# GeGLU down products of both sequence halves in the second pass, with the first half's hidden tiles stored in HBM

## The chip, the cores and the metric

The kernel runs on one core of one Trainium2 chip. The metric is the device time of one launch in microseconds (us). The kernel before takes 787.78 us, the median of 3 runs (787.53 to 787.96). The profile is of one further execution.

## The reference

The input x has 2048 rows of 512 numbers. It is normalized row by row, and two branches are added to it: a Fourier mixing written as products with DFT matrices, and a gated feed-forward layer (GeGLU) with 1792 hidden columns.

```python
    a = jnp.einsum("bsd,ed->bse", x, dft_hid_re)
    b = jnp.einsum("bsd,ed->bse", x, dft_hid_im)
    y = jnp.einsum("ts,bse->bte", dft_seq_re, a) - jnp.einsum("ts,bse->bte", dft_seq_im, b)
    ...
    g = jnp.einsum("bsd,df->bsf", x, w_gate)
    u = jnp.einsum("bsd,df->bsf", x, w_up)
    h = _gelu(g) * u
    return jnp.einsum("bsf,fd->bsd", h, w_down)
    ...
    return x + _A_ref(xn, ...) + _B_ref(xn, ...)
```

Everything is fp32.

## The kernel before

Each fp32 operand is split into two parts in a reduced fp32 format, a high part (a copy on ScalarE, line 295, tile names ending in h) and a low part (a subtraction on VectorE, line 300, names ending in l). A product is then three matmuls (`mm3`, line 311): high by high and the two mixed ones. Block products are done by a scheme with seven products in place of eight (numbered 0, 1, 4, 5, 6, 2, 3), whose results pass through PSUM banks in a chain: products accumulate in a bank, the bank's running sum is copied out by ScalarE (`copy`, line 1620), and a later product goes on accumulating in the same bank. A full matmul is 128 by 128 by 512, and a `W` of the code, one product of a unit, is six of them.

The first half of the program makes the Fourier branch (tiles named z, m, y). The second half, `units`, makes the feed-forward layer in 28 units. Unit n makes gate columns (n even) or up columns (n odd) of pair q = n // 2, 256 hidden columns for one half of the sequence: units 0 to 13 are the first pass (rows 0 to 1023), units 14 to 27 the second pass (rows 1024 to 2047). A unit has banks a, b and c. Product 5 accumulates in b, ScalarE copies b to a side tile q6, product 6 accumulates in b, ScalarE copies b to a side tile w, and product 3 closes b. In the first pass an even unit also makes inner products, `X` (three matmuls each, banks b2 and c2), which both passes share; they are written to HBM (`m_park`) and start the second pass's banks from there.

When a pair's gate and up blocks are there, ScalarE applies the gelu (`gate`, line 747) and VectorE multiplies (`up_1`, line 752): four hidden tiles s per pair. From these, VectorE and ScalarE form the seven operands of the down product (`hl`, names hh, hl, hth, htl). The down weights of pair q (`wd`, loaded at line 677) are summed (`weight_sums`, line 642) and split in the same way, for each q of 0 to 13, though q and q + 7 use the same weights.

Down products (`down_op`, tiles dn) are small PE jobs of three matmuls for each pair q in them. `TURNS` says which pairs are multiplied together in one bank: `[[0], [1, 2], [3, 4], [5, 6], [7, 8, 9], [10, 11], [12, 13]]`. When a turn's last pair is ready, its 14 jobs go to a list `todo`, and `fill` places them between the products of the units that follow, at the places that `order(n)` marks with d0 to d3. A finished dn bank is copied by ScalarE to a tile `part` (line 1704) and added to an HBM tensor `partial` by a DMA on GpSimd's queue (line 1707). The last turn (`last_down`) starts its banks from `partial` and stores the output.

The order of the PE's instructions is the order in which `add` is called with engine "p". A planner in the kernel (class `Plan`) places the other engines' operations around it, by assumed costs and by the room in a pool of 109 tiles of 128 by 512 fp32 in SBUF (`SLOTS`) and 8 PSUM banks.

```python
            if lead(n - 1, 4):
                return "5 Y43 1 d1 Y42 d2 6 d0 3 d3 2"
            if fetched(n, 4):
                return "5 1 d2 6 d0 3 d1 2 d3"
```

These strings give the order in a unit: digits are products, X and Y inner products (Y42 and Y43 are the last two of the unit ahead), d a place for down jobs. The first is that of an odd unit of the first pass, the second that of a unit of the second pass.

Of the kernel before, what the change touches and what calls it, by code (L numbers as in the profile page):

```python
# [261 lines left out]
def fnet_geglu_kernel(ctx: ExitStack, tc: tile.TileContext, x, xt, cs, dh, wgu, wd, out):  # L262
# [81 lines left out]
    m_park = dram.tile([2, NP, 2, P, CH], F32, name="m_park")  # L344
    x_park = dram.tile([2, 2, P, CH], F32, name="x_park")
# [976 lines left out]
    TURNS = [[0], [1, 2], [3, 4], [5, 6], [7, 8, 9], [10, 11], [12, 13]]  # L1322
    INNER_AHEAD = 2
    INTO_ACC = (6, 3)
# [27 lines left out]
    def unit_at(n):  # L1352
        return TU + n * 14.25
# [76 lines left out]
    def units():  # L1430

        def weights(m):
            name, at = m if isinstance(m, tuple) else (0, m)
            if short(m):
                add(("lw", m), "s", .9, lambda: load_short(m), mb=MB, makes={("wx", m): 1})
            else:
                add(("lw", m), "s", .9, lambda: load_w(m) if isinstance(m, int) else load_wd(m[1]), mb=2 * MB, makes={("wx", m): 2},
                    ahead=W_AHEAD if (m if isinstance(m, int) else 2 * m[1]) < NP - 2 else None)
# [41 lines left out]
        for q in range(NP):  # L1480
            weights(("d", q))
# [200 lines left out]
        def down_op(qs, r, js):  # L1682
            sp, key = qs[0] // (NP // 2), (qs[0], r, js[0])
            tiles = {}

            def f():
                for j in js:
                    tiles[j] = ps_tile("dn")
                    down_product(qs, r, j, tiles[j])
            k = {0: 0, 1: 0, 4: 1, 5: 1, 6: 2, 2: 2, 3: 3}[r]  # L1690
            add(("dn", *key), "p", 3 * MM * len(js) * len(qs), f,
                after=[("lo", ("w", ("d", q), k)) for q in qs] + [("lo", ("h", q, r)) for q in qs],
                uses=[("wl", ("d", q), k) for q in qs] + [("hl", q, r) for q in qs], banks=[("dn", qs[0], r, j) for j in js],
                holds=[("dn", qs[0], r, j) for j in js])
            for j in js:
                if qs == TURNS[-2] and r in INTO_ACC:
                    add(("dc", qs[0], r, j), "v", V5, lambda j=j: nc.vector.tensor_add(acc[r, j], tiles[j], acc[r, j]),
                        after=[("dn", *key), ("la", 2, r, j)], uses=[("acc", 2, r, j)], holds=[("dn", qs[0], r, j)])
                    continue
                part = {}  # L1700

                def cp(j=j, part=part):
                    part[0] = slot("part")
                    nc.scalar.activation(part[0], tiles[j], AF.Copy)  # L1704
                add(("dc", qs[0], r, j), "a", A5, cp, after=[("dn", *key)], makes={("part", qs[0], r, j): 1}, holds=[("dn", qs[0], r, j)])
                sent = [("da", qs[0] - 1, r, j)] if qs[0] % (NP // 2) else [("lys", 3, j)] if sp and r == 3 else []
                add(("da", qs[-1], r, j), "g", .6, lambda j=j, part=part: nc.gpsimd.dma_start(partial[sp, r, j], part[0], accum_op=OP.add),  # L1707
                    after=[("dc", qs[0], r, j), *sent], uses=[("part", qs[0], r, j)], mb=MB, adds=True)

        def more(q):  # L1710
            for qs in TURNS[:-1]:
                if q == qs[-1]:
                    todo.extend(("d", qs, r, [j]) for r in D_ORDER for j in range(2))
                    return [2 * t[-1] + 2 for t in TURNS if t[-1] > q][0]
# [6 lines left out]
        def hidden(n, blk, ready, src, holds, uses):  # L1721
# [5 lines left out]
            add(("f", n, blk), "v", V5, lambda: up_1(n, blk, src()), after=[*ready, ("f", n - 1, blk)], holds=holds, uses=[*uses, s], soon=2 if holds else SOON)  # L1727
            if blk in H_USE:
                r = H_USE[blk]
                add(("hi", ("h", q, r)), "a", A5, lambda: up_2(n, blk), after=[("f", n, blk)], uses=[s], makes={("hl", q, r): 2})  # L1730
                add(("lo", ("h", q, r)), "v", V5, lambda: up_3(n, blk), after=[("hi", ("h", q, r))], uses=[s, ("hl", q, r)])

        def hidden_sums(q):
            s = [("s", q, blk) for blk in H_PLACE]
            n = 2 * q + 1
            f = [("f", n, blk) for blk in H_PLACE]
            for k, (after, uses) in enumerate((([f[0], f[1]], [0, 1]), ([("hs", q, 0), f[3], ("lo", ("h", q, 2))], [3, 1]),
                                               ([("hs", q, 1), ("lo", ("h", q, 0))], [3, 0]), ([("hs", q, 1), f[2], ("lo", ("h", q, 1))], [2, 3]))):
                add(("hs", q, k), "v", V5, lambda k=k: h_sum(q, k), after=after, uses=[s[u] for u in uses])
# [3 lines left out]
        for q in range(NP - 1):  # L1743
            hidden_sums(q)

        turn = 4

        def order(n):
# [14 lines left out]
        for n in range(U1):  # L1763
            if n % 2 == 0:
                turn = more(n // 2 - 1) or turn
            wanted = -(-len(todo) // (turn - n))
# [12 lines left out]
            for u in order(n).split():  # L1779
                if u[0] == "d":  # L1780
# [4 lines left out]
                else:  # L1785
                    mult(n, int(u))
# [10 lines left out]
                    elif u == "2":  # L1797
                        sums("aq", n, "q6", "c", [("p", n, 2), ("q6", n)], c)
                        hidden(n, (0, 1), [("aq", n)], lambda n=n: side[n, "q6"], [], [("q6", n)])
# [3 lines left out]
        def last_down(qs):  # L1803

            sp, tiles, p0 = NC // 2 - 1, {}, {}
            given = TURNS[-2]

            def step(r, j, *h):
                k, sl = (r, j, *h), slice(h[0] * HD, (h[0] + 1) * HD) if h else slice(CH)
                hold, a = ("dn", "z", *k), ("acc", 2, r, j)  # L1810

                def seed():
                    tiles[k] = ps_tile("dn")[:, :HD if h else CH]
                    nc.scalar.activation(tiles[k], acc[r, j][:, sl], AF.Copy)
                add(("es", *k), "a", A2 if h else A5, seed, after=[("la", 2, r, j), ("dc", given[0], r, j)], uses=[a], banks=[hold], holds=[hold])
                w = {0: 0, 1: 0, 4: 1, 5: 1, 6: 2, 2: 2, 3: 3}[r]
                add(("e", *k), "p", (1.5 if h else 3) * MM * len(qs), lambda: down_product(qs, r, j, tiles[k], True, sl),
                    after=[("es", *k)] + [("lo", ("w", ("d", q), w)) for q in qs] + [("lo", ("h", q, r)) for q in qs],
                    uses=[("wl", ("d", q), w) for q in qs] + [("hl", q, r) for q in qs], holds=[hold])
                done, u = ("zd", *k), ("p0", j)  # L1820
# [10 lines left out]
                if r == 0:  # L1831
                    def first():
                        p0[j] = slot("p0")
                        nc.scalar.activation(p0[j], tiles[k], AF.Copy)
                    drain(first, [], [], {u: 1}, "a", A5)
                elif r == 2:
                    drain(lambda: nc.scalar.activation(acc[2, j], tiles[k], AF.Copy), [], [a], (), "a", A5)
                elif r == 1:
                    drain(lambda: nc.vector.tensor_add(acc[1, j], tiles[k], p0[j]), [("zd", 0, j)], [a, u])
                    put((0, 0), lambda: acc[1, j], a, done)  # L1840
                elif r == 5:
                    drain(lambda: plus(p0[j]), [("zd", 1, j)], [u])
                    add(("z5", j), "v", V5, lambda: nc.vector.tensor_add(acc[2, j], acc[2, j], p0[j]), after=[done, ("zd", 2, j)],
                        uses=[u, ("acc", 2, 2, j)])
                elif r == 4:
                    drain(lambda: plus(acc[2, j]), [("z5", j)], [("acc", 2, 2, j)])
                    put((0, 1), lambda: acc[2, j], ("acc", 2, 2, j), done)
                elif r == 6:
                    drain(lambda: plus(p0[j]), [("z5", j)], [u])
                    add(("z6", j), "v", V5, lambda: nc.vector.tensor_add(acc[4, j], tiles[4, j], p0[j]), after=[done, ("e", 4, j)],  # L1850
                        uses=[u, ("acc", 2, 4, j)], holds=[("dn", "z", 4, j)])
                    put((1, 1), lambda: acc[4, j], ("acc", 2, 4, j), ("z6", j))
                elif not h:
                    drain(lambda: plus(p0[j]), [("z6", j)], [u])
                    put((1, 0), lambda: p0[j], u, done)
                else:
                    def end():
                        nc.vector.tensor_add(p0[j][:, sl], tiles[k], p0[j][:, sl])
                        (nc.sync if h[0] else nc.scalar).dma_start(out[2 + j, 2 * sp, :, sl], p0[j][:, sl])
                    drain(end, [("z6", j)], [u], (), "v", V2)  # L1860

            for r in D_ORDER[:-1]:
                for j in range(2):
# [77 lines left out]
```

## Time and profile before

| what | value |
|---|---|
| median of 3 runs | 787.78 us |
| the profiled execution's own time | 787.55 us |
| span from the first to the last instruction | 785.8 us |
| PE busy | 781.2 us, 99% |
| VectorE (DVE) busy | 743.7 us, 95% |
| ScalarE (ACT) busy | 555.8 us, 71% |
| matmuls | 3441 |
| HBM read, written | 127.14 MB, 74.73 MB |

Busy time of a PE is modelled, since matmuls overlap: a row gives a matmul 0.39 us, while the next one starts sooner. The start times of successive matmuls tell the pace. The profiled time is 1.75 us above its span, and 0.23 us below the median.

### The profile page before, as it was taken

Reading aid. Unit: us, or ns where it says so; the run is one execution under the profiler, and the core shown is the slowest. Engines: PE = TensorE matmul, PEld = TensorE weight load, DVE = VectorE, ACT = ScalarE, POOL = GpSimd, SP = SyncE. Lnnn points to the kernel's source line nnn. Section 1 sums busy time; section 2 is a strip of 40 time slices with the busy share of each in tenths; the row PEclk is TensorE's granted clock in tenths of the full one; section 3 lists DMA queues with packets and bytes.
Section 4 is the critical chain, followed back from the end, with each engine's and each line's share of the span. In section 5 each row is a group of like instructions: output and inputs, shape, how many; then the busy total and the mean of one; then the engine's idle time right before and its main releaser. Section 6 shows DMA issues by size and latency. Waiting matters only on the chain.

```text
span 785.8 us, 11798 instructions
## 1 busy us (share of the span) xinstructions
PE 781.2 (99%) x3441; PEld 644.3 (82%) x3441; DVE 743.7 (95%) x1415; ACT 555.8 (71%) x1057; POOL 177.5 (23%) x268
## 2 busy tenths in 40 slices
PE   9999999999999999999999999999999999999998
PEld 6888888888888888888888888888888888888886
DVE  7999999999899899999999998999999999999986
ACT  6997555666545374766777776787787898878863
POOL 0110520043221042000222431343322212222200
PEclk9999999999999999999999999999999999999999
DMA  9976997779999879982765986697799984999952
GB/s 331 388 192 171 367 352 267 248 278 273 359 371 373 315 297 375 393 315 84 197 216 137 209 187 150 121 314 153 200 255 348 290 208 81 283 324 247 247 131 108
DMA packets 103377, 199.52 MB, mean 254 GB/s; under 512 B 12272, under 2 KB 21520, under 8 KB 103120
## 3 DMA queue, kind: packets, MB, share of 16 engines
q1 hardware_dynamic: 75600, 129.81, 47.8%
q0 software_dynamic: 27424, 68.70, 35.6%
q8 instruction: 27, 0.44, 0.2%
q14 instruction: 38, 0.31, 0.1%
q10 hardware_dynamic: 288, 0.26, 0.1%
HBM read 127.14 MB, written 74.73 MB: 257 GB/s over the span
## 4 chain that ended last, share of the span: by engine, by line
PE 96%; DMA 1%; issue 1%; POOL 1%; ACT 0%; DVE 0%; POOLq 0%; ACTq 0%
PE m L311 35%; PE b L311 19%; PE dn L311 16%; PE y L311 10%; PE c L311 7%; PE a L311 5%; PE z L311 4%; DMA partial<-part 1%; DMA x<-in_x 0%; POOL partial L1707 0%; POOL xT_hl L625 0%; POOL m_park L1628 0%; ACT part L1704 0%; DVE bn L378 0%; ACT q L1620 0%
## 5 line engine op out<-in xcount | busy, mean ns | idle before, releaser
L295 ACT ACTIVATE psh<-pan 128x512 fp32r<-128x512 f32 x203 | 118.0, 625 | 73.7 <-DVE pan L587 23.2
L300 DVE TENSOR_TENSOR psl<-pan,psh 128x512 fp32r<-128x512 f32 x198 | 128.6, 681 | 0.3 <-ACT psh L295 0.2
L1707 POOL DMA_DIRECT2D partial<-part x80 | 69.5, 876 | 187.1 <-ACT part L1704 147.0
L311 PE MATMUL m<-psh,xcl 128*128 128x512 f32 x232 | 90.2, 389 | 0.0
L311 PE MATMUL m<-psh,xch 128*128 128x512 f32 x232 | 90.2, 389 | 0.0
L311 PE MATMUL m<-psl,xch 128*128 128x512 f32 x232 | 90.2, 389 | 0.0
L1704 ACT ACTIVATE part<-dn 128x512 f32<-128x512 f32 x80 | 47.3, 594 | 17.4 <-PE dn L311 16.8
L311 PEld LDWEIGHTS m<-psh,xch 128*128 128x128 f32 x232 | 43.6, 188 | 9.1
L311 PEld LDWEIGHTS m<-psh,xcl 128*128 128x128 f32 x232 | 43.5, 188 | 9.1
L311 PEld LDWEIGHTS m<-psl,xch 128*128 128x128 f32 x232 | 43.6, 188 | 8.9
L300 DVE TENSOR_TENSOR wl<-ws,wh 128x512 fp32r<-128x512 f32 (+1 forms) x70 | 46.3, 671 | 3.3 <-ACT wh L295 3.2
L295 ACT ACTIVATE wh<-ws 128x512 fp32r<-128x512 f32 (+1 forms) x70 | 42.3, 615 | 0.6 <-DVE ws L642 0.6
L552 POOL DMA_DIRECT2D partial<-part x28 | 20.7, 765 | 95.6 <-ACT part L548 81.1
L587 DVE TENSOR_TENSOR pan<-pan 128x512 f32<-128x512 f32 x58 | 38.8, 682 | 2.6 <-DMA pan<-in_cs 2.6
L311 PE MATMUL m<-psh,xa 128*128 128x512 f32 x116 | 40.4, 389 | 0.0
L300 DVE TENSOR_TENSOR htl<-s,hth 128x512 fp32r<-128x512 f32 x56 | 37.8, 685 | 2.2 <-ACT hth L295 2.2
L1620 ACT ACTIVATE w<-b 128x512 f32<-128x512 f32 x42 | 25.1, 599 | 18.8 <-PE b L311 17.8
L1058 POOL DMA_DIRECT2D t_park<-pan x29 | 16.1, 556 | 95.0 <-DVE pan L588 84.1
L765 DVE TENSOR_TENSOR s<-s 128x512 f32<-128x512 f32 x56 | 37.3, 684 | 0.1
L1620 ACT ACTIVATE q<-b 128x512 f32<-128x512 f32 x42 | 25.1, 597 | 15.7 <-PE b L311 13.9
L295 ACT ACTIVATE hth<-s 128x512 fp32r<-128x512 f32 x56 | 33.8, 627 | 1.4 <-DVE s L765 1.3
L311 PE MATMUL dn<-hth,wh 128*128 128x512 f32 x84 | 32.7, 389 | 0.0
(761 smaller groups left out, 2424.5 us busy)
## 6 DMA issues: line engine op xcount, KB each, us to landing
pan<-in_cs SPq DMA_DIRECT2D x157, 256.0 KB, 6.3
partial<-part POOLq DMA_DIRECT2D x108, 256.0 KB, 5.6
wx<-in_wgu SPq DMA_DIRECT2D x48, 256.0 KB, 5.3
t_park<-pan POOLq DMA_DIRECT2D x29, 256.0 KB, 5.9
pan<-t_park SPq DMA_DIRECT2D x29, 256.0 KB, 5.9
wd<-in_wd SPq DMA_DIRECT2D x28, 256.0 KB, 5.8
m<-m_park SPq DMA_DIRECT2D x28, 256.0 KB, 6.4
acc<-partial SPq DMA_DIRECT2D x28, 256.0 KB, 4.6
```

What stands on the lines that cost most here:

```text
L295: nc.scalar.activation(t[0], src, AF.Copy, scale=float(sign))
L300: engine.tensor_sub(t[1], src, hi)
L311: nc.tensor.matmul(ps, a[u][:, sl], b[v], start=first and r == 0, stop=last and r == 2, skip_group_check=resumed)
L552: nc.gpsimd.dma_start(partial[sp, r, j], ypart.pop((r, j)), **({} if r in (0, 5, 6) else {"accum_op": OP.add}))
L587: return [lambda: nc.vector.tensor_sub(t3, b22, b12), lambda: nc.vector.tensor_sub(t1, b12, b11), lambda: (nc.vector.tensor_sub(b22, *((t1 ...
L765: nc.vector.tensor_sub(t, u, v)
L1058: plan.add(("park", i), "g", .6, lambda: nc.gpsimd.dma_start(t2_park[c, k], pan_src[i][5]), after=[("S", i, 2)], mb=MB, uses=[("r", i, b22)])
L1620: nc.scalar.activation((bank if banks else side)[(n, to, *more)], src(), AF.Copy)
L1704: nc.scalar.activation(part[0], tiles[j], AF.Copy)
L1707: add(("da", qs[-1], r, j), "g", .6, lambda j=j, part=part: nc.gpsimd.dma_start(partial[sp, r, j], part[0], accum_op=OP.add), after=[("dc" ...
```

## The change

All down products are made in the second pass. `TURNS` now names pairs of weights, `[[0, 1], [2, 3], [4, 5, 6]]`, and a turn's jobs are made for both halves of the sequence (q = p and q = p + 7) from one prepared set of weights. The first pass writes its 28 hidden tiles s to HBM (`h_park`, GpSimd's queue) as soon as they are multiplied, and the second pass loads them again (SP's queue) and forms the operands there. Units 4 to 18 have no down jobs to place; turn 0 starts at unit 19, turn 1 at unit 23, and the last turn, 28 jobs for three pairs, follows unit 27. The strings of `order` are changed for odd units of the first pass and for the second pass (z is product 2 of the unit ahead). A planner's function for due times (`unit_at`) and the separate final sums of the first half are replaced to match.

```diff
+    h_park = dram.tile([NP // 2, 4, P, CH], F32, name="h_park")
...
-            mm3(ps, wl[("d", q), r], cols(j), [t[:, part] for t in hl[q, r]], q == qs[0] and not seeded, q == qs[-1],
+            mm3(ps, wl[("d", q % (NP // 2)), r], cols(j), [t[:, part] for t in hl[q, r]], q == qs[0] and not seeded, q == qs[-1],
...
-    TURNS = [[0], [1, 2], [3, 4], [5, 6], [7, 8, 9], [10, 11], [12, 13]]
+    TURNS = [[0, 1], [2, 3], [4, 5, 6]]
+    BEGIN = [4, 19, 23]
...
-        for q in range(NP):
+        for q in range(NP // 2):
             weights(("d", q))
...
+            if n < NP:
+                add(("hp", q, blk), "g", .6, lambda: nc.gpsimd.dma_start(h_park[q, H_PLACE.index(blk)], hs[q, blk]), after=[("f", n, blk)],
+                    uses=[s], mb=MB)
+
+                def get():
+                    hs[q, blk] = slot("s")
+                    nc.sync.dma_start(hs[q, blk], h_park[q, H_PLACE.index(blk)])
+                add(("hg", q, blk), "s", .45, get, after=[("hp", q, blk)], makes={("s2", q, blk): 1}, mb=MB)
...
             if lead(n - 1, 4):
-                return "5 Y43 1 d1 Y42 d2 6 d0 3 d3 2"
+                return "5 Y43 d1 6 1 d2 3 d0 Y42 " + "2 " * (n < NP - 1) + "d3"
...
             if fetched(n, 4):
-                return "5 1 d2 6 d0 3 d1 2 d3"
+                return "5 1 d2 6 " + "z " + "d0 3 d1 d3" + " 2" * (n == U1 - 1)
...
-            if n % 2 == 0:
-                turn = more(n // 2 - 1) or turn
-            wanted = -(-len(todo) // (turn - n))
+            if n in BEGIN[1:]:
+                t = BEGIN.index(n) - 1
+                todo.extend(("d", t, sp, r, j) for r in D_ORDER for sp in range(2) for j in range(2))
+            wanted = -(-len(todo) // (min(b for b in (*BEGIN, U1) if b > n) - n))
...
+            for r in (0, 2, 1, 5):
+                for sp in range(2):
+                    for j in range(2):
+                        step(r, sp, j)
...
+        while todo:
+            fill()
         last_down(TURNS[-1])
```

Three places show how instructions move. Buffer numbers stand behind the names.

The first is PE in unit 4, an even unit of the first pass (a, c: banks of its outer products; xT00, xT40, xT01: inputs of inner products; dn: a down job). Before:

```order
L311 MATMUL a_5221<-xT00h_3971,wh_5118 128x512
L311 MATMUL a_5221<-xT00l_3972,wh_5118 128x512
L311 MATMUL a_5221<-xT00h_3971,wl_5119 128x512
L311 MATMUL c_5227<-xT40h_4160,wh_5130 128x512
L311 MATMUL c_5227<-xT40l_4161,wh_5130 128x512
L311 MATMUL c_5227<-xT40h_4160,wl_5131 128x512
L311 MATMUL dn_5236<-hth_5110,wh_5072 128x512
L311 MATMUL dn_5236<-hth_5110,wl_5073 128x512
L311 MATMUL dn_5236<-htl_5111,wh_5072 128x512
L311 MATMUL a_5221<-xT01h_3982,wh_5118 128x512
```

And now:

```order
L311 MATMUL a_5170<-xT00h_3978,wh_5073 128x512
L311 MATMUL a_5170<-xT00l_3979,wh_5073 128x512
L311 MATMUL a_5170<-xT00h_3978,wl_5074 128x512
L311 MATMUL c_5177<-xT40h_4117,wh_5078 128x512
L311 MATMUL c_5177<-xT40l_4118,wh_5078 128x512
L311 MATMUL c_5177<-xT40h_4117,wl_5079 128x512
L311 MATMUL a_5170<-xT01h_4000,wh_5073 128x512
L311 MATMUL a_5170<-xT01l_4001,wh_5073 128x512
```

Bank a is copied by ScalarE between its third matmul and its fourth. The down job that stood there is gone: three matmuls on another bank are left between the two. It is so in units 4, 6, 8, 10 and 12.

The second is PE in unit 5, an odd unit (b: the bank of products 5, 6 and 3). Before, the rows ahead of these are the last of product 5 on b, three of b2 (inner product 3) and the first five of product 1 (on the bank b2 of its own):

```order
L311 MATMUL b2_5233<-xT11h_4112,wl_5248 128x512
L311 MATMUL dn_5465<-hth_5325,wh_5012 128x512
L311 MATMUL dn_5465<-hth_5325,wl_5013 128x512
L311 MATMUL dn_5465<-htl_5326,wh_5012 128x512
L311 MATMUL c2_5339<-xT41h_4702,wih_5267 128x512
L311 MATMUL c2_5339<-xT41l_4703,wih_5267 128x512
L311 MATMUL c2_5339<-xT41h_4702,wil_5268 128x512
L311 MATMUL dn_5482<-hth_5325,wh_5012 128x512
L311 MATMUL dn_5482<-hth_5325,wl_5013 128x512
L311 MATMUL dn_5482<-htl_5326,wh_5012 128x512
L311 MATMUL b_5387<-xT60h_4147,wh_5350 128x512
```

And now, from the last of product 5 to the first of product 6:

```order
L311 MATMUL b_5297<-xT51h_4191,wl_5125 128x512
L311 MATMUL b2_5187<-xi43h_4692,wh_5124 128x512
L311 MATMUL b2_5187<-xi43l_4693,wh_5124 128x512
L311 MATMUL b2_5187<-xi43h_4692,wl_5125 128x512
L311 MATMUL b_5297<-xT60h_4099,wh_5138 128x512
```

Between product 5 and product 6 on bank b, with the copy q6 to be made in between, there were 18 matmuls and there are three now. It is so in units 5, 7, 9, 11 and 13.

The third is ACT at the copy q6 of unit 5 (part: copy of a dn bank; s: a gelu; w2, q6, b: copies of banks). Before:

```order
L1620 ACTIVATE q2_5401<-b2_5240 128x512
L1704 ACTIVATE part_5418<-dn_5409 128x512
L1620 ACTIVATE w2_5430<-b2_5240 128x512
L295 ACTIVATE wh_5433<-wx_5319 128x512
L1620 ACTIVATE q6_5442<-b_5387 128x512
```

And now:

```order
L1621 ACTIVATE q2_5317<-b2_5187 128x512
L295 ACTIVATE wh_5321<-ws_5252 128x384
L295 ACTIVATE wh_5327<-ws_5289 128x512
L295 ACTIVATE w_5334<-wx_5198 128x256
L1621 ACTIVATE w2_5343<-b2_5187 128x512
L748 ACTIVATE s_5346<-q6_5225 128x512
L1621 ACTIVATE q6_5353<-b_5297 128x512
```

A gelu of the unit ahead now stands directly in front of the copy q6; it does so in all five odd units.

## Rows read from the trace of the kernel before

**Rows 1.** The page, part 1: busy us, share of the span, instructions.
```profile
PE 781.2 (99%) x3441; PEld 644.3 (82%) x3441; DVE 743.7 (95%) x1415; ACT 555.8 (71%) x1057; POOL 177.5 (23%) x268
```

**Rows 2.** The page, part 4: the chain of waits, shares by engine.
```profile
PE 96%; DMA 1%; issue 1%; POOL 1%; ACT 0%; DVE 0%; POOLq 0%; ACTq 0%
```

**Rows 3.** The chain in order of time: start us, us, what.
```profile
97.39 76.16 PE m L311 x336
```

**Rows 4.** Timeline, unit 5: start us, us, instruction, [idle before it <- releaser].
```profile
465.56 0.39 PE L311 MATMUL b<-xT61h,wl 128*128 128x512 f32 x1
465.78 0.61 PE L311 MATMUL dn<-hth,w 128*128 128x512 f32 x2
465.98 0.60 ACT L1620 ACTIVATE w<-b 128x512 f32<-128x512 f32 x1 [0.69 <-PE b L311]
...
466.63 0.50 PE L311 MATMUL b<-xT30h,w 128*128 128x512 f32 x1
...
466.97 0.39 PE L311 MATMUL b<-xT30l,w 128*128 128x512 f32 x1
...
468.13 0.62 PE L311 MATMUL dn<-hth,w 128*128 128x512 f32 x2
```

**Rows 5.** Timeline, unit 8: the second pause of PE, and ACT ahead of it.
```profile
522.10 0.60 ACT L1620 ACTIVATE q<-b 128x512 f32<-128x512 f32 x1 [1.13 <-DMA partial<-part]
...
522.30 0.39 PE L311 MATMUL c<-xT21h,wl 128*128 128x512 f32 x1
...
522.75 0.50 PE L311 MATMUL b<-xi46h,wih 128*128 128x512 f32 x1
...
525.64 0.39 PE L311 MATMUL b<-xT10h,wh 128*128 128x512 f32 x1
```

**Rows 6.** Timeline, unit 3: a copy with six matmuls between.
```profile
436.32 0.39 PE L311 MATMUL b<-xT61h,wl 128*128 128x512 f32 x1
...
436.74 0.60 ACT L1620 ACTIVATE w<-b 128x512 f32<-128x512 f32 x1 [0.76 <-PE b L311]
...
437.68 0.39 PE L311 MATMUL dn<-hl,wh 128*128 128x512 f32 x1
...
437.90 0.39 PE L311 MATMUL b<-xT30h,w 128*128 128x512 f32 x1
```

**Rows 7.** Windows: busy us (x instructions) of PE, PEld, DVE, ACT, POOL; PEclk, DMA share, GB/s.
```profile
460.00:480.00 20.00, 19.99 (x89) 16.23 (x88) 19.23 (x41) 15.47 (x31) 5.84 (x8) 1.00 0.61 106
520.00:540.00 20.00, 19.94 (x88) 16.14 (x88) 18.85 (x44) 14.45 (x28) 8.51 (x15) 1.00 0.89 246
```

**Rows 8.** Groups by line and form: busy us, mean ns of one | idle before.
```profile
L642 DVE TENSOR_TENSOR ws<-wd 128x256 f32<-128x256 f32 x28 | 11.1, 418 | 0.0
L300 DVE TENSOR_TENSOR wl<-ws,wh 128x512 fp32r<-128x512 f32 x63 | 42.4, 684 | 2.8 <-ACT wh L295 2.7
L295 ACT ACTIVATE wh<-ws 128x512 fp32r<-128x512 f32 x63 | 38.7, 626 | 0.6 <-DVE ws L642 0.6
L1704 ACT ACTIVATE part<-dn 128x512 f32<-128x512 f32 x80 | 47.3, 594 | 17.4 <-PE dn L311 16.8
L747 ACT ACTIVATE s<-q 128x512 f32<-128x512 f32 x14 | 8.8, 630 | 2.7 <-DVE q L1624 2.6
```

**Rows 9.** The page, part 6: DMA issues, KB each, median us to landing.
```profile
wx<-in_wgu SPq DMA_DIRECT2D x48, 256.0 KB, 5.3
m<-m_park SPq DMA_DIRECT2D x28, 256.0 KB, 6.4
```

**Rows 10.** Timeline, the end: matmuls of half width.
```profile
780.88 0.28 PE L311 MATMUL dn<-htl,w 128*128 128x256 f32 x1
...
781.24 0.28 PE L311 MATMUL dn<-htl,w 128*128 128x256 f32 x1
```

**Rows 11.** Timeline, the start: PE's warm-up matmuls.
```profile
0.78 4.00 PE L806 MATMUL warm<-const-bfloat16-1.0 128*128 128x512 bf16 x9 [0.78 <-PEq L1934]
```

More of the change, by code (lines that the diff above doesn't have):

```diff
@@ L1680, in late @@
                 add(("lys", r, j), "g", .6, lambda: y_send(1, r, [j]), after=[("lyc", r, j)], uses=[("lp", r, j)], mb=MB, adds=r == 3)
-        def down_op(qs, r, js):
-            sp, key = qs[0] // (NP // 2), (qs[0], r, js[0])
-            tiles = {}
-            def f():
[L1687 to L1714, printed above, removed]
+        W_OF = {0: 0, 1: 0, 4: 1, 5: 1, 6: 2, 2: 2, 3: 3}
+        def at(sp, ps):
+            return [p + sp * NP // 2 for p in ps]
+        def down_op(t, sp, r, j):
+            ps = TURNS[t]
+            qs, key, hold = at(sp, ps), (t, sp, r, j), ("dn", t, sp, r, j)
+            tile_, part = [], []
+            def f():
+                tile_.append(ps_tile("dn"))
+                down_product(qs, r, j, tile_[0])
+            def cp():
+                part.append(slot("part"))
+                nc.scalar.activation(part[0], tile_[0], AF.Copy)
+            add(("dn", *key), "p", 3 * MM * len(qs), f, after=[("lo", ("w", ("d", p), W_OF[r])) for p in ps] + [("lo", ("h", q, r)) for q in qs],
+                uses=[("wl", ("d", p), W_OF[r]) for p in ps] + [("hl", q, r) for q in qs], banks=[hold], holds=[hold])
+            add(("dc", *key), "a", A5, cp, after=[("dn", *key)], makes={("part", *key): 1}, holds=[hold])
+            sent = [("da", t - 1, sp, r, j)] if t else [("lys", r, j) if r in (5, 3) else ("yd", r)] if sp else []
+            add(("da", *key), "g", .6, lambda: nc.gpsimd.dma_start(partial[sp, r, j], part[0], accum_op=OP.add),
+                after=[("dc", *key), *sent], uses=[("part", *key)], mb=MB, adds=True)
@@ L1726, in hidden @@
                 return
[L1727 to L1731, printed above, removed]
@@ L1733, in hidden_sums @@
-        def hidden_sums(q):
-            s = [("s", q, blk) for blk in H_PLACE]
-            n = 2 * q + 1
-            f = [("f", n, blk) for blk in H_PLACE]
+            add(("f", n, blk), "v", V5, lambda: up_1(n, blk, src()), after=[*ready, ("f", n - 1, blk)], holds=holds, uses=[*uses, s],
+                soon=2 if holds else SOON)
+            if n < NP:
[5 more added lines that the diff above has]
+                add(("hg", q, blk), "s", .45, get, after=[("hp", q, blk)], makes={("s2", q, blk): 1}, mb=MB)
@@ new lines, in hidden_sums @@
+        def hidden_sums(q):
+            n, parked = 2 * q + 1, 2 * q < NP
+            s = [("s2" if parked else "s", q, blk) for blk in H_PLACE]
+            f = [("hg", q, blk) if parked else ("f", n, blk) for blk in H_PLACE]
+            for blk, r in H_USE.items():
+                i = H_PLACE.index(blk)
+                add(("hi", ("h", q, r)), "a", A5, lambda blk=blk: up_2(n, blk), after=[f[i]], uses=[s[i]], makes={("hl", q, r): 2})
+                add(("lo", ("h", q, r)), "v", V5, lambda blk=blk: up_3(n, blk), after=[("hi", ("h", q, r))], uses=[s[i], ("hl", q, r)])
@@ L1741, in hidden_sums @@
                 split_of(("h", q, r), lambda k=k: h_split(q, k), [("hs", q, k)], [s[(1, 3, 0, 2)[k]]], {("hl", q, r): 2})
-        for q in range(NP - 1):
+        for q in range(NP):
             hidden_sums(q)
-        turn = 4
         def order(n):
@@ L1797, in units, with last_down, load, step @@
                     elif u == "2":
-                        sums("aq", n, "q6", "c", [("p", n, 2), ("q6", n)], c)
-                        hidden(n, (0, 1), [("aq", n)], lambda n=n: side[n, "q6"], [], [("q6", n)])
+                        sums("aq", m, "q6", "c", [("p", m, 2), ("q6", m)], spot(m, "c"))
+                        hidden(m, (0, 1), [("aq", m)], lambda m=m: side[m, "q6"], [], [("q6", m)])
             sums("aw", n, "w", "c", [("w", n)] + [x for x in ready_c if x in plan.ops], c)
             hidden(n, (1, 1), [("aw", n)], lambda n=n: side[n, "w"], [], [("w", n)])
[L1803 to L1810, printed above, removed]
+        def last_down(ps):
+            tiles, p0 = {}, {}
+            last = len(TURNS) - 2
+            def load(sp, r, j):
+                acc[sp, r, j] = slot("acc")
+                nc.sync.dma_start(acc[sp, r, j], partial[sp, r, j])
+            def step(r, sp, j, *h):
+                k, sl = (sp, r, j, *h), slice(h[0] * HD, (h[0] + 1) * HD) if h else slice(CH)
+                qs = at(sp, ps)
+                hold, a, v = ("dn", "z", *k), ("acc", sp, r, j), acc
+                if not h or not h[0]:
+                    add(("la", sp, r, j), "s", .45, lambda: load(sp, r, j), after=[("da", last, sp, r, j)], makes={a: 1}, mb=MB)
@@ L1812, in seed @@
                 def seed():
                     tiles[k] = ps_tile("dn")[:, :HD if h else CH]
-                    nc.scalar.activation(tiles[k], acc[r, j][:, sl], AF.Copy)
-                add(("es", *k), "a", A2 if h else A5, seed, after=[("la", 2, r, j), ("dc", given[0], r, j)], uses=[a], banks=[hold], holds=[hold])
-                w = {0: 0, 1: 0, 4: 1, 5: 1, 6: 2, 2: 2, 3: 3}[r]
+                    nc.scalar.activation(tiles[k], v[sp, r, j][:, sl], AF.Copy)
+                add(("es", *k), "a", A2 if h else A5, seed, after=[("la", sp, r, j)], uses=[a], banks=[hold], holds=[hold])
@@ L1848, in step @@
                 elif r == 6:
[L1849 to L1852, printed above, removed]
+                    drain(lambda: plus(p0[s]), [("z5", *s)], [u])
+                    add(("z6", *s), "v", V5, lambda: nc.vector.tensor_add(v[sp, 4, j], tiles[sp, 4, j], p0[s]), after=[done, ("e", sp, 4, j)],
+                        uses=[u, ("acc", sp, 4, j)], holds=[("dn", "z", sp, 4, j)])
@@ L1891, in units @@
-        for r in range(7):
-            for j in range(2):
-                add(("la", 2, r, j), "s", .45, lambda r=r, j=j: load_acc(1, r, j), after=[("da", TURNS[-3 if r in INTO_ACC else -2][-1], r, j)],
-                    makes={("acc", 2, r, j): 1}, mb=MB)
-        hidden_sums(NP - 1)
+                        nc.vector.tensor_add(p0[s][:, sl], tiles[k], p0[s][:, sl])
+                        (nc.sync if h[0] else nc.scalar).dma_start(out[2 + j, 2 * sp, :, sl], p0[s][:, sl])
+                    drain(end, [("z6", *s)], [u], (), "v", V2)
```

78 lines of the change are left out of this document (33 added, 45 removed).

## The prediction

> **What bounds the kernel now.** I read the page's busy times first [rows 1], then the chain [rows 2, 3], then single pauses in the timeline [rows 4 to 6]. The busy row says that TensorE (PE) works 99% of the span, VectorE 95%, ScalarE 71%. The chain says the same more strongly: 96% of it runs through PE. A row of it shows the pace, 76.16 us for 336 matmuls, or 0.2267 us each [rows 3]. So a change counts if it adds or removes matmuls, or makes PE wait. Work taken off the other engines counts only where PE waits for it.
>
> In the second half of the program I found two places where successive matmuls start further apart than this pace allows. In unit 5 the last matmul of product 6 starts at 465.56; ScalarE's copy of that bank starts 0.42 later, at 465.98; product 3, on the same bank, starts at 466.63, 0.65 after the copy's start [rows 4]. So from the bank's last matmul to its next one 1.07 us pass (0.42 + 0.65), of which three down matmuls between fill only to 4 x 0.2267 = 0.91: a wait of 0.16. The restart is slow as well: 466.63 to 466.97 is 0.34 for one matmul. From 465.78 to 468.13 nine matmuls take 2.35 where 9 x 0.2267 = 2.04 is the pace, so such a place costs **0.31 us**. The reader is to compare it with unit 3: the same bank, with six matmuls between, 436.32 to 437.90 [rows 6]. That is 1.58 = 7 x 0.2267, no loss at all, and the copy again starts 0.42 after its matmul.
>
> The other place is in unit 8: the copy starts at 522.10 after 1.13 idle us, held by a DMA that adds to `partial`, and PE restarts at 522.75, 0.65 after the copy's start [rows 5]. From 522.30 to 525.64 are 13 matmuls, 3.34 against 13 x 0.2267 = 2.95, a loss of 0.39.
>
> **The change, part by part.**
>
> *Matmuls.* The down product has the same terms in both programs. What differs is how the last ones are cut: three full matmuls fewer, six of half width more. Half-width ones start 0.12 apart (780.88 to 781.24 is three) [rows 10]. 6 x 0.12 - 3 x 0.2267 = **+0.04**.
>
> *VectorE and ScalarE.* Preparing each pair once drops 28 half-width sums (28 x 0.418 = 11.7 us) and 28 subtractions (at most 28 x 0.684 = 19) on VectorE, and 28 copies on ScalarE (at most 28 x 0.626 = 18) [rows 8]. Fewer turns drop 24 of the 80 copies of dn banks (24 x 0.594 = 14), while the last turn's 14 more seeds put 8 back. VectorE also loses 14 final sums and gains some 10 in the last turn. Together that is some 30 us less for VectorE and 20 for ScalarE. On PE's path it is **zero**: neither engine stands in the chain now (0% each, [rows 2]), and where they have time left over PE cannot go faster than its pace.
>
> *The two old pauses.* Both owe their place to first-pass down work: the short fill in unit 5, and the full pool behind the `partial` DMA in unit 8. With no down jobs there, products 6 and 3 have product 1 between them (six matmuls), and no `part` tile is needed in these units. I take both as gone, **-0.70**. This is also all that the second half has to give: 0.09% of the time.
>
> *New short distances.* With the fills gone, 15 places have three matmuls between a bank's copy and its next product, against one before. In units 4, 6, 8, 10 and 12 the copy after X00 has X40 for cover; the one after X40 has X01, and is covered by the pause that the first has already made, so I count one pause in each unit. In units 5, 7, 9, 11 and 13 the copy q6 has only Y43 for cover. That is ten places of 0.31 or more. In the even units I take 5 x 0.31 = **+1.55**, with the copy issued at once, as in [rows 4]. In the odd units a gelu stands directly in front of q6 on ScalarE, 0.63 us long [rows 8]. If it has ended when the bank is ready the price is 0.31, if it has just begun 0.94. The gelu's own input is ready earlier, when product 2 of the unit ahead has been summed, so I take a quarter of its length, 0.16: 5 x 0.47 = **+2.35**. The bounds of the ten are 3.1 and 6.25; below 3.1, if only the wait of 0.16 is lost and the slow restart is made up, 1.6.
>
> *Moved transfers.* The 28 stores of hidden tiles join GpSimd's queue where 24 additions leave it. The queue is idle most of the time (23% busy, [rows 1]), so zero. The 28 loads join SP's queue, where 14 loads of down weights leave. A 256 KB load takes 5.3 to 6.4 us from issue to landing [rows 9], and the DMA engines are 61 to 89% busy [rows 7]. What is queued behind a late hidden tile is VectorE, in order: the subtractions of the weights of the next unit, and PE behind them. I take zero, since units 4 to 18 have no down jobs and the tiles can come at leisure; without that lead one wait costs up to 5.3 us. A gain is excluded: PE waits for no load there now.
>
> *The clock.* PE was granted full speed, 2.4 GHz, in both stretches with pauses (1.00, [rows 7]), so short pauses cost only themselves and this term is zero. The Trainium skill ("TensorE: Matmul & The Clock Gate", section "A second HAM failure mode: psum-queue depth-cycling") speaks against this change: it describes a kernel whose PE idles briefly between groups of matmuls, often enough that the clock swings between its two levels and throughput falls. By that rule ten regular pauses could cost more than their sum; two isolated pauses in these rows neither agree nor refute it.
>
> *Sum.* 787.55 (the profiled execution, 1.75 above its span) + 0.04 - 0.70 + 1.55 + 2.35 = 790.79. The median of the runs lies 0.23 above that execution, so I say **791.0 us**, +0.4%.
>
> **The rivals.**
>
> *The pauses cost half (not slower).* Mechanism: ScalarE, 20 us lighter, meets each bank at once, and PE's later matmuls make up for the slow restart; then each of the ten costs the 0.16 wait alone: 1.6 + 0.04 - 0.70 = +0.94, 788.7 us. The same comes out if one of the two kinds does not pause. It decides for "no change" as long as the ten together stay below 2.3 (1.6 + 0.66). For it: at 466.63 one restart alone was measured. Against: nine matmuls after it nothing had been made up.
>
> *No pauses at all.* If the fills were not needed, as where six matmuls stand between and nothing is lost [rows 6], the old pauses go and nothing comes: 787.78 + 0.04 - 0.70 = 787.1. Against: [rows 4] is the very distance that now comes 15 times, and it paused.
>
> *The gelu holds q6 fully.* ScalarE runs in order, and its order is fixed when the program is built. If the sum before the gelu arrives late, all of it stands in the way: 5 x 0.94 + 1.55 - 0.66 = 5.6, 793.4 us. For it: the gelu is in that place five times out of five.
>
> *A late load.* VectorE is held once by a hidden tile or a weight, 5.3 us, on top of the pauses: 791.0 + 5.3 = 796.3. For it: the DMA share of 0.89. Against: nothing of this kind stands in the chain now.
>
> *The clock falls.* In the cold start nine matmuls took 4.00 us, 0.44 each [rows 11], which is the lower level, 1.2 GHz. If PE ran at it in units 4 to 13 for as little as 20 us, 10 us of work would be put off: 801 us. Against: 1.00 in [rows 7]. The rule named above would lead here.
>
> **How the numbers follow.** Two runs of one kernel can be told apart at about 0.2%, here 1.6 us, so faster means below 786.2 and slower above 789.4. Chances: the forecast 0.50; half price 0.17; the gelu holds 0.18; a late load 0.07; the clock 0.03; no pauses 0.05. The forecast, the held gelu, the late load and the clock are slower: 0.78. Half price is within the bound, as is most of "no pauses" (at 787.1 it is 0.1% off): 0.17 + 0.03 = 0.20; 0.02 is left for faster, since all that PE can give back is 0.70. The range runs from 788.5, which takes in half price, to 795.0, above the held gelu and short of the late load: it leaves out the load, the clock and "no pauses", 0.15.
>
> **What would show it.** Right: in the timeline of the changed kernel, PE pauses ahead of X01 in the even units 4 to 12 and ahead of product 6 in the odd units 5 to 13, each with a copy of that bank ending in it and an interval of about 0.34 behind it; no pause between 6 and 3 in unit 5; VectorE some 30 us less busy, ScalarE 20 less; matmuls 3444. A gelu that ends within 0.4 us of the q6 copy's start points to the dearer price. Wrong: PE's starts at an even pace through units 4 to 13, a pause in units 14 to 18 or in the last turn, or a clock below 1.00 anywhere behind the start.

## The result and the profile after

The changed kernel takes **789.53 us** (median of 12 runs, 789.26 to 790.47); beside it the kernel before took 787.87 (12 runs, 787.34 to 788.97). The ratio is 1.0021, with a 95% interval of 1.0012 to 1.0030: slower, by 1.7 us.

The page of the changed kernel, parts 1 and 4, answers to [rows 1, 2]:

```profile
PE 783.1 (99%) x3444; PEld 643.0 (82%) x3444; DVE 717.5 (91%) x1355; ACT 539.2 (68%) x1023; POOL 171.7 (22%) x272
...
PE 99%; DMA 0%; DVE 0%; ACT 0%; issue 0%; ACTq 0%
```

VectorE has 26 us less to do and ScalarE 17, and the program is longer all the same: the chain is PE, now 99% of it. Pauses of 0.3 us do not show in its shares; they are seen in the start times of PE's matmuls. Behind the start, and one spot at 88 us that both kernels have, there are exactly ten places where matmuls start over 0.30 us apart, and they are the ten that the forecast named. This is the one in unit 4 (timeline; PE and ScalarE):

```profile
437.17 0.39 PE L311 MATMUL a<-xT00h,wl 128*128 128x512 f32 x1
437.40 0.39 PE L311 MATMUL c<-xT40h,wh 128*128 128x512 f32 x1
437.60 0.58 ACT L1621 ACTIVATE b<-a 128x512 f32<-128x512 f32 x1 [2.07 <-PE a L311]
...
437.85 0.39 PE L311 MATMUL c<-xT40h,wl 128*128 128x512 f32 x1
...
438.23 0.50 PE L311 MATMUL a<-xT01h,wh 128*128 128x512 f32 x1
...
438.56 0.39 PE L311 MATMUL a<-xT01l,wh 128*128 128x512 f32 x1
```

It is the pattern of [rows 4]. The copy of bank a starts 0.43 us after the bank's last matmul, PE's next one on it 0.63 after the copy: 1.06 us, where four starts at the pace fill 0.91. The restart takes 0.33 in place of 0.23. And the one in unit 7, where the gelu stands in front of the copy q6:

```profile
476.51 0.63 ACT L748 ACTIVATE s<-q 128x512 f32<-128x512 f32 x1
...
476.95 0.39 PE L311 MATMUL b<-xT51h,wl 128*128 128x512 f32 x1
...
477.38 0.60 ACT L1621 ACTIVATE q<-b 128x512 f32<-128x512 f32 x1 [0.24 <-PE b L311]
...
477.63 0.39 PE L311 MATMUL b<-xi43h,wl 128*128 128x512 f32 x1
...
478.02 0.50 PE L311 MATMUL b<-xT60h,wh 128*128 128x512 f32 x1
478.36 0.40 PE L311 MATMUL b<-xT60l,wh 128*128 128x512 f32 x1
```

The idle time in the row of the copy is what decides the open term of the forecast: ScalarE had finished the gelu 0.24 us before the bank was ready. The releaser named in brackets is PE's bank, not the gelu. It is so in all five odd units (0.24 to 0.30 idle where a row gives it; in unit 9 the gelu starts 0.71 before the copy and takes 0.64).

To price all ten alike I take the time from the matmul before a pause to at most 16 matmuls on, less that many times 0.2267. The even units give 0.33 each, the odd ones 0.37, 0.30, 0.30, 0.30 and 0.31: 3.23 together. The pauses of [rows 4, 5] are gone (0.31 and 0.39 by the same count).

Two small differences lie outside, at the ends. PE's first product started 0.25 earlier because a load of x landed earlier (the first VectorE row that waits for it, before and then after):

```profile
3.62 0.75 DVE L378 BATCH_NORM_STATS2 bn<-x 128x6 f32<-128x256 f32 x2 [2.75 <-DMA x<-in_x]
...
4.57 0.74 PE L808 MATMUL warm<-const-bfloat16-1.0 128*128 128x128 bf16 x5
...
5.45 1.08 PE L311 MATMUL z<-panh,xa 128*128 128x512 f32 x2
6.36 0.63 PE L311 MATMUL z<-panh,xb 128*128 128x512 f32 x2
```

```profile
3.37 0.75 DVE L379 BATCH_NORM_STATS2 bn<-x 128x6 f32<-128x256 f32 x2 [2.50 <-DMA x<-in_x]
...
4.50 0.45 PE L809 MATMUL warm<-const-bfloat16-1.0 128*128 128x128 bf16 x5
...
5.20 0.73 PE L311 MATMUL z<-panh,xa 128*128 128x512 f32 x2 [0.25 <-DVE xa L402]
...
5.77 0.63 PE L311 MATMUL z<-panh,xb 128*128 128x512 f32 x2
```

In the profile before, PE also came up to its pace later: the last five warm-up matmuls take 0.74 against 0.45, and the first two matmuls of z 0.91 (5.45 to 6.36) against 0.57. The time that PE loses in the first 20 us is 2.77 before and 2.24 after, and between 2.17 and 3.04 in all twelve profiles of this study, whatever was changed: I put this 0.53 down to chance. At the end, from the start of the last matmul to the end of the span, 3.82 us pass before and 3.44 after. The run order_alone (below), the kernel before with one order changed, has 3.83, and all variants of the changed one 3.43 or 3.44, unless they carry more traffic (3.72, 3.73). So 0.38 is a gain of the change, in the landing of the last stores; why was not tried.

The profile's account closes: 0.04 - 0.70 + 3.23 - 0.53 - 0.38 = +1.66, and the spans are 785.78 and 787.44.

### The profile page after: what moved, and what is told of

Its sections match the earlier page's. It is cut to its first block, busy times and chain, and to the rows that moved or that the text cites. A ratio compares the mean times of both kernels' runs of the same rounds, so it can differ in the third digit from the quotient of the medians.

```text
span 787.4 us, 11752 instructions
## 1 busy us (share of the span) xinstructions
PE 783.1 (99%) x3444; PEld 643.0 (82%) x3444; DVE 717.5 (91%) x1355; ACT 539.2 (68%) x1023; POOL 171.7 (22%) x272
## 4 chain that ended last, share of the span: by engine, by line
PE 99%; DMA 0%; DVE 0%; ACT 0%; issue 0%; ACTq 0%
PE m L311 35%; PE b L311 21%; PE dn L311 17%; PE y L311 10%; PE c L311 7%; PE a L311 5%; PE z L311 4%; DMA x<-in_x 0%; DVE bn L379 0%; ACT q L1621 0%; DVE p L1870 0%; DVE xa L402 0%; ACT w L390 0%; DVE stats L381 0%; PE st L1245 0%
## 5 line engine op out<-in xcount | busy, mean ns | idle before, releaser
L1704 POOL DMA_DIRECT2D partial<-part x56 | 48.9, 872 | 118.1 <-ACT part L1699 79.3
L1699 ACT ACTIVATE part<-dn 128x512 f32<-128x512 f32 x56 | 33.3, 596 | 13.2 <-PE dn L311 12.9
L300 DVE TENSOR_TENSOR wl<-ws,wh 128x512 fp32r<-128x512 f32 (+1 forms) x56 | 37.3, 670 | 4.6 <-ACT wh L295 4.4
L553 POOL DMA_DIRECT2D partial<-part x28 | 20.8, 789 | 79.5 <-ACT part L549 73.2
L295 ACT ACTIVATE wh<-ws 128x512 fp32r<-128x512 f32 (+1 forms) x56 | 33.6, 611 | 0.0
L311 PE MATMUL dn<-hh,wh 128*128 128x512 f32 x84 | 32.7, 389 | 0.0
```

Source lines behind the costliest of these rows:

```text
L295: nc.scalar.activation(t[0], src, AF.Copy, scale=float(sign))
L300: engine.tensor_sub(t[1], src, hi)
L311: nc.tensor.matmul(ps, a[u][:, sl], b[v], start=first and r == 0, stop=last and r == 2, skip_group_check=resumed)
L553: nc.gpsimd.dma_start(partial[sp, r, j], ypart.pop((r, j)), **({} if r in (0, 5, 6) else {"accum_op": OP.add}))
L1699: nc.scalar.activation(part[0], tile_[0], AF.Copy)
L1704: add(("da", *key), "g", .6, lambda: nc.gpsimd.dma_start(partial[sp, r, j], part[0], accum_op=OP.add), after=[("dc", *key), *sent], uses=[ ...
```

## The experiments

Theory: PE pauses because three matmuls do not cover the copy of a bank. Rivals: A, the gelu holds the copy; B, the traffic of the hidden tiles is the price; C, each stop at a copied bank has a fixed price; D, the new order itself makes the pauses. Each variant ran 4 to 11 times beside the kernel before, and the ratios are to that. The changed kernel was not timed again with them; the kernel before took 787.20 to 787.81 in these sessions and 787.87 beside the changed kernel, so a difference from 789.53 can be off by up to 0.7 us.

**odd_spaced: six matmuls on either side of product 6.**

```diff
-                return "5 Y43 d1 6 1 d2 3 d0 Y42 " + "2 " * (n < NP - 1) + "d3"
+                return "5 1 d1 6 Y43 Y42 d2 3 d0 " + "2 " * (n < NP - 1) + "d3"
```

> The odd units run 5, product 1, 6, Y43, Y42, 3: six matmuls between products 5 and 6 and six between 6 and 3; nothing else is touched. Theory (PE pauses because three matmuls do not cover the copy of the bank): the five pauses ahead of product 6 vanish, the five ahead of X01 stay, PE gets back 5 x 0.31 = 1.6 us, 788.0 us. Rival A (the copy q6 is held on ScalarE by the gelu, whatever stands between): pauses stay, 789.5. Rival B (the 1.7 us are the price of the stores and loads of the hidden tiles, and PE makes up its pauses elsewhere): 789.5.

Measured: 788.13 us (before 787.81; ratio 1.0006, 0.9997 to 1.0015), 1.4 less than the changed kernel. The five odd pauses are gone, the five even ones are there, 0.33 each. The gelu still stands in front of q6 and the traffic is the same, so A and B fail as they were stated. Six matmuls would also hide a gelu that held the copy for up to 0.5 us; that it holds nothing at all is shown by the idle time ahead of the copies (0.21 to 0.30 in the rows of this run too).

**odd_none: nothing between products 5 and 6.**

```diff
-                return "5 Y43 d1 6 1 d2 3 d0 Y42 " + "2 " * (n < NP - 1) + "d3"
+                return "5 d1 6 Y43 1 d2 3 d0 Y42 " + "2 " * (n < NP - 1) + "d3"
```

> The odd units run 5, 6, Y43, 1, 3: no matmul at all stands between products 5 and 6. Theory (the pause is what is missing to 1.07 us from a bank's last matmul to its next one, plus 0.15 of slow restart): each of the five costs 1.07 - 0.23 + 0.15 = 0.99 us in place of 0.31, 5 x 0.68 = 3.4 us more, 792.9 us. Rival C (a fixed price for each stop of PE at a bank that has just been copied): no change, 789.5. Rival A (the gelu holds the copy): between the two, since the copy then waits for the gelu, 0.63 us long.

Measured: 794.53 us (ratio 1.0088, 1.0074 to 1.0102). Timeline, unit 5:

```profile
454.62 0.39 PE L311 MATMUL b<-xT51h,wl 128*128 128x512 f32 x1
455.04 0.60 ACT L1621 ACTIVATE q<-b 128x512 f32<-128x512 f32 x1 [0.24 <-PE b L311]
...
455.69 0.50 PE L311 MATMUL b<-xT60h,wh 128*128 128x512 f32 x1 [0.69 <-ACT q L1621]
456.03 0.40 PE L311 MATMUL b<-xT60l,wh 128*128 128x512 f32 x1
```

Again 0.42 and 0.65, 1.07 together. The five cost 0.98, 0.98, 0.98, 1.05 and 0.98, against 0.99 expected: not a fixed price (C). Of the 4.9 us by which the span is longer than the changed kernel's, 3.4 are these; 0.86 are three pauses elsewhere (333, 384 and 413 us), where the planner, which places everything anew for each order, put other work; the rest lies at the start.

**double_copy: the copy q6 made twice in the odd units.**

```diff
-                nc.scalar.activation((bank if banks else side)[(n, to, *more)], src(), AF.Copy)
+                for _ in range(1 + twice):
+                    nc.scalar.activation((bank if banks else side)[(n, to, *more)], src(), AF.Copy)
...
-                        copy("q6", n, "q6", lambda n=n: bank[n, "b"], [("p", n, 5)], holds=[b])
+                        copy("q6", n, "q6", lambda n=n: bank[n, "b"], [("p", n, 5)], holds=[b], twice=lead(n - 1, 4))
```

> In the changed kernel the copy q6 of the units 5, 7, 9, 11 and 13 is made twice, one after the other, to the same tile. Theory (PE waits for the time at which ScalarE lets the bank go): a second copy starts 0.50 us behind the first, so each of the five pauses is 0.50 longer, 789.5 + 2.5 = 792.0 us. Rival C (a fixed price for a stop): 789.5. This is also the price of a gelu that would hold the copy by 0.50.

Measured: 792.54 us (ratio 1.0062, 1.0049 to 1.0076).

```profile
453.71 1.23 ACT L1622 ACTIVATE q<-b 128x512 f32<-128x512 f32 x2 [0.24 <-PE b L311]
...
454.99 0.50 PE L311 MATMUL b<-xT60h,wh 128*128 128x512 f32 x1 [0.64 <-ACT q L1622]
```

PE restarts 1.28 after the start of the pair, 0.63 later than with one copy, and the five pauses grow from between 0.30 and 0.37 to between 0.94 and 0.97, by 0.57 in unit 5 and by 0.64 to 0.66 in the others. So the added delay on ScalarE at this place lands on PE; that a second copy to the same tile takes 0.63 and not 0.50 was not expected. A gelu that held the copy would therefore have had its price on PE. It does not hold it.

**even_inner: another order of inner products in the even units.**

```diff
-                return "X00 X40 d1 X01 X41 X04 5 1 X05 d2 6 X06 X44 d0 3 X03 X02 X45 2 d3 X46"
+                return "X00 X40 X04 d1 X01 X41 X44 5 1 d2 6 X05 X45 d0 3 X06 2 X03 d3 X46 X02"
```

> The even units 4 to 12 run their inner products in another order, with six matmuls or more between every copy of a bank and its next product; the odd units keep their five short places. Theory: the five pauses ahead of X01 vanish, the five ahead of product 6 stay, 789.5 - 1.6 = 787.9 us. Rival B (transfers): 789.5.

Measured: 796.72 us (ratio 1.0120, 1.0102 to 1.0138), far from 787.9, so as a test it is a miss. From unit 4 on the theory's pauses are as expected: none ahead of X01, five ahead of product 6 (0.30 to 0.37). But this order applies to units 0 and 2 too, and the planner places the other engines' work anew for each order. New pauses between 245 and 422 us, 1.1, 0.4, 2.3, 1.0, 0.8 and 0.9 among them, cost more than was won. One brought something else; windows of this run around it (busy us of PE, PEld, DVE, ACT, POOL, then the granted clock):

```profile
383.40:385.80 2.40, 0.39 (x3) 0.01 (x1) 2.31 (x6) 1.78 (x4) 0.00 (x0) 1.00 1.01 120
385.80:387.06 1.26, 1.26 (x6) 1.04 (x6) 1.26 (x3) 1.23 (x3) 0.92 (x2) 1.00 0.94 169
387.06:390.40 3.34, 3.34 (x9) 2.59 (x8) 2.81 (x6) 2.83 (x6) 0.22 (x1) 0.50 0.43 159
```

PE was idle for 2.0 us, ran at full clock for five matmuls, and was then granted half of it (1.2 GHz) for 3.3 us: matmuls 0.43 apart, some 1.6 us more. **both_inner**, the same with the new odd order, ended the same way.

> Both new orders at once, no place with fewer than six matmuls between. Theory: none of the ten pauses is left, 789.5 - 3.2 = 786.3 us, which is 1.6 below the kernel before, more than the 0.7 that its own two pauses cost it. If the two parts only add where PE is the bound all along, the two single runs' gains sum to this one's. Rival B (transfers): 789.5.

Measured: 794.93 us (ratio 1.0094, 1.0080 to 1.0108). No pause from unit 4 on, the same cluster at 384 us and others before it. It is 1.8 less than even_inner, about what five pauses cost, but the other pauses differ between the two runs as well (one of 1.6 us at 333 us is in this one alone), so the additive reading is not tested by it.

**even_spaced: product 2 of the unit ahead as cover behind X40.**

```diff
-                return "X00 X40 d1 X01 X41 X04 5 1 X05 d2 6 X06 X44 d0 3 X03 X02 X45 2 d3 X46"
+                return "X00 X40 " + "z " * lead(n - 2, 4) + "d1 X01 X41 X04 5 1 X05 d2 6 X06 X44 d0 3 X03 X02 X45 2 d3 X46"
...
-                return "5 Y43 d1 6 1 d2 3 d0 Y42 " + "2 " * (n < NP - 1) + "d3"
+                return "5 Y43 d1 6 1 d2 3 d0 Y42 " + "2 " * (not lead(n + 1, 4) and n < NP - 1) + "d3"
```

> In units 6, 8, 10 and 12 product 2 of the unit ahead moves behind X40, so nine matmuls stand between X00 and X01; unit 4 keeps three, and so do the odd units ahead of product 6. Theory: four of the ten pauses vanish, 4 x 0.33 = 1.3 us less than the changed kernel, 788.2 us. Rival B (transfers): 789.5. The run with the other order of inner products did not decide this, since it also changed the first half of the program.

Measured: 788.06 us (ratio 1.0005, 0.9997 to 1.0014), 1.5 less than the changed kernel (1.2 if each is taken against the kernel before beside it). The expectation is wrong in one thing: the condition holds in unit 4 as well, so five pauses go and not four (5 x 0.33 = 1.65, 787.9). The odd ones stay.

**both_spaced: both.** The same even order, and the odd one of odd_spaced, with product 2 moved in the same way.

> The odd order with six matmuls on either side of product 6, and the even order with product 2 of the unit ahead behind X40. Theory: one pause of the ten is left, in unit 4; 789.5 - 5 x 0.31 - 4 x 0.33 = 786.7 us, faster than both kernels, 1.1 below the one before. Rival B (transfers): 788 to 789.5, the gain of the odd order at most.

Measured: **786.25 us** (11 runs; before 787.56; ratio 0.9983, 0.9974 to 0.9992), faster than both kernels. None of the ten pauses is left: behind the spot at 88 us no two matmuls start over 0.30 apart. These are the places in units 4 and 5, ahead of X01 and of product 6:

```profile
436.41 0.39 PE L311 MATMUL a<-xT00h,wl 128*128 128x512 f32 x1
...
436.83 0.58 ACT L1621 ACTIVATE b<-a 128x512 f32<-128x512 f32 x1
...
438.67 0.39 PE L311 MATMUL a<-xT01h,wh 128*128 128x512 f32 x1
438.90 0.39 PE L311 MATMUL a<-xT01l,wh 128*128 128x512 f32 x1
...
453.41 0.39 PE L311 MATMUL b<-xT51h,wl 128*128 128x512 f32 x1
...
453.89 0.60 ACT L1621 ACTIVATE q<-b 128x512 f32<-128x512 f32 x1 [0.30 <-PE b L311]
...
454.99 0.39 PE L311 MATMUL b<-xT60h,wh 128*128 128x512 f32 x1
455.22 0.39 PE L311 MATMUL b<-xT60l,wh 128*128 128x512 f32 x1
```

The copies start 0.42 and 0.48 after their matmul, and nine and six matmuls stand between: 436.41 to 438.67 is 10 and 453.41 to 454.99 is 7 starts at the pace. With unit 4 counted, 789.53 - 1.58 - 1.65 = 786.3.

So the change proper, without its short places, is worth 1.3 us, of which the profile explains 0.70 by the old pauses and 0.38 by the end (the spans, 785.78 and 784.83, differ by 0.95: these two, less 0.04 for the matmuls and 0.09 at the start).

**order_alone: the kernel before with the new odd order.**

```diff
-                return "5 Y43 1 d1 Y42 d2 6 d0 3 d3 2"
+                return "5 Y43 d1 6 1 d2 3 d0 Y42 2 d3"
```

> The kernel before, with the new order of its odd units alone: down products stay in the first pass and fill the places d0 to d3, so no copy of a bank has fewer than six matmuls behind it. Theory (the pauses come from the fills that are gone, not from the new order): no pause ahead of product 6 or X01, the one of unit 5 gone as well, 787.2 to 787.6 us, not slower than before. Rival D (the new order itself makes the pauses): five pauses in the odd units, 787.9 + 1.6 = 789.5.

Measured: 790.74 us (ratio 1.0045, 1.0033 to 1.0058). From unit 4 to the end of the first pass there is no pause at all, so the order does not make them where down jobs fill (D fails), as expected. That it is slower was not. Its pauses are others, 1.7 at 412 us and 0.5, 1.0 and 0.8 at 629, 639 and 726. The second of the three:

```profile
637.43 0.39 PE L311 MATMUL b<-xT61h,wl 128*128 128x512 f32 x1
...
638.76 0.63 ACT L295 ACTIVATE hh<-s 128x512 fp32r<-128x512 f32 x1 [0.76 <-DVE s L752]
...
639.29 0.58 ACT L1620 ACTIVATE w<-b 128x512 f32<-128x512 f32 x1
...
639.92 0.50 PE L311 MATMUL b<-xT30h,w 128*128 128x512 f32 x1 [0.75 <-ACT w L1620]
```

Here six matmuls stand between, and the copy is late nonetheless: ScalarE stands at a split that waits for VectorE, and the copy is behind it. This is the mechanism of the held copy, with another holder.

**double_park: every hidden tile stored twice and loaded twice into the same tile.**

```diff
+                    nc.gpsimd.dma_start(h_park2[q, H_PLACE.index(blk)], hs[q, blk])
                     nc.gpsimd.dma_start(h_park[q, H_PLACE.index(blk)], hs[q, blk])
...
+                    nc.sync.dma_start(hs[q, blk], h_park2[q, H_PLACE.index(blk)])
                     nc.sync.dma_start(hs[q, blk], h_park[q, H_PLACE.index(blk)])
```

> Every hidden tile of the first pass is written to HBM twice, to two places, and loaded twice into the same tile: 28 stores and 28 loads of 256 KB more. Theory (transfers are hidden): 789.5 us, and the ten pauses as they were. Rival B (the added transfers are the price of the change): as much again as the change added, 789.5 + 1.7 = 791.2 us or more, with new pauses of PE behind unit 14.

Measured: 826.62 us (ratio 1.0486, 1.0459 to 1.0513). Waits of the SP queue (in all, times, longest):

```profile
SPq L1731 <- DMA s<-h_park: 120.6, 28, 10.1
```

The second load of a tile waits on the queue for the first to land, 28 times, 4.3 us on average, and every load behind it waits too. PE's pauses in the second pass grow to 5.8 us, with spells at half the clock behind the longest (granted 0.66 from 673 to 680 us). So this run did not test the traffic. Its first half tested the stores: with the stores doubled, the ten pauses are as they were (0.30 to 0.33) and no other stands between 434 and 586 us.

**double_traffic: more traffic, no tile waited for twice.** Against double_park, the second load is replaced by a copy from HBM to HBM.

```diff
-                    nc.sync.dma_start(hs[q, blk], h_park2[q, H_PLACE.index(blk)])
                     nc.sync.dma_start(hs[q, blk], h_park[q, H_PLACE.index(blk)])
+                    nc.sync.dma_start(h_park3[q, H_PLACE.index(blk)], h_park2[q, H_PLACE.index(blk)])
```

> The changed kernel, with every hidden tile stored a second time to another place in HBM, and every load followed by a copy of that second place from HBM to HBM on the same queue, which nothing waits for: the traffic of the stores and loads at least doubled, with no tile waited for twice. Theory (traffic is hidden; it was the second wait for each tile on the in-order queue of SP that cost 37 us in the run with double loads): 789.5 us, ten pauses. Rival B (the traffic is a price): above 791.

Measured: 792.22 us (ratio 1.0055, 1.0041 to 1.0068; 790.4 to 793.7). So the 789.5 expected here was missed. The ten pauses are the same, and seven more come in the second pass, 3.3 us in all. Ahead of the largest, 1.45 us at 643 us, ScalarE has waited for two hidden tiles:

```profile
639.07 0.63 ACT L295 ACTIVATE hh<-s 128x512 fp32r<-128x512 f32 x1 [4.72 <-DMA s<-h_park]
...
641.10 0.63 ACT L295 ACTIVATE hh<-s 128x512 fp32r<-128x512 f32 x1 [0.35 <-DMA s<-h_park]
```

Over the whole run such waits of ScalarE (in all, times, longest) are, in the changed kernel and then here:

```profile
ACT hh L295 <- DMA s<-h_park: 1.7, 1, 1.7
```

```profile
ACT hh L295 <- DMA s<-h_park: 11.9, 8, 4.7
```

A load of a hidden tile takes 6.7 us from issue to landing in the changed kernel and 8.3 here (medians). So the traffic that the change adds is hidden, since both_spaced has it all and no pause; this much more is not. Whether the added copies cost by their bytes or by their place on SP's queue, ahead of other loads, was not tried.

## Why the prediction was right, and where it was off

- *Side and mechanism.* Slower, and by the pauses forecast, in the ten places and in no others. The measured 789.53 lies in the range, between the forecast of 791.0 and the half-price rival of 788.7, and nearer the rival: the time alone does not tell the two apart. The trace does. That rival's mechanism did not occur: the slow restart is lost each time, and both kinds pause. It is luck, too, that the time passes the prediction's own mark for slower, 789.4, by 0.1; the ten pauses do not depend on that.
- *The size.* In the profiles the sum of the terms was 3.24 and 1.66 came out: -0.77 from the odd units, +0.10 from the even ones, -0.53 at the start and -0.38 at the end.
- *The old pauses and the matmuls.* -0.70 and +0.04, as forecast.
- *Even units.* 1.55 forecast, 5 x 0.33 = 1.65 measured.
- *Odd units: the term that was mis-sized.* "I take a quarter of its length, 0.16": the gelu's part was 0. The sum said 2.35 and the trace gives 1.58. The gelu's place in the order says that it can hold the copy; when its input is ready decides whether it does. Product 2 of the unit ahead ends before product 5 starts; in unit 7 the gelu then starts 0.87 before the copy, and it needs 0.63. The prediction's sign for the dearer price, a gelu that ends within 0.4 us of the copy's start, was met in all five units while the price was the cheap one: a gelu may end just ahead of the copy and hold nothing.
- *Cover.* No price for 26 us less on VectorE and 17 less on ScalarE: right.
- *The end.* The last stores land 0.38 earlier; the forecast had nothing for it, and its cause stays open.
- *Late load.* It cost PE nothing, though ScalarE once waited 1.7 us for a hidden tile, and it was nearer than its chance of 0.07 suggests: loads waited for on SP's queue, or the traffic of double_traffic, bring it. In that run it was ScalarE, at the split hh, that the late tile held first, where the prediction named VectorE.
- *The clock.* It was granted at 1.00 in units 4 to 13: ten pauses of 0.3 us did not move it. The swing of the clock by frequent short idle times between groups of matmuls, which the Trainium skill describes for another kernel ("TensorE: Matmul & The Clock Gate", section "A second HAM failure mode: psum-queue depth-cycling"), did not come about here. A fall to half the clock did follow a single pause of 2.0 us in even_inner, and one as long in both_inner; after one of 1.8 us in double_park (at 587 us) the clock stayed at 1.00.

## What to carry to other kernels

Where PE is the bound, list the places where a bank is read and then written again, and count the matmuls between: on this kernel 1.07 us pass from the start of a bank's last matmul, by way of ScalarE's copy, to the start of its next one, so three matmuls between lose 0.3 us, and six lose nothing if the copy is not held. Filler work has a second use as cover; whoever moves it away must put other work in its place, as both_spaced does, or the saving elsewhere is paid back on PE. What stands ahead of a copy on its engine is a risk only if it is still waiting or running when the bank is ready, and that is read from the idle time, and its releaser, in the row of the copy.

## What was not expected of the hardware

In even_inner, after 2.0 us of idle, PE ran five matmuls at 2.4 GHz before the clock fell to 1.2 for 3.3 us. A second copy to the same tile on ScalarE ended 0.63 us after the first, where other operations on it follow each other at 0.50 (476.01 to 476.51 in unit 7). In double_park a second load into a tile stood on the queue for 4.3 us on average until the first had landed.
